# A fused attention and FFN kernel with a written issue order: every engine's order rewritten, and one wait named in the last pair's results

## The chip, the cores and the metric

The kernel runs on one core of one Trainium2 chip, as a single program. The metric is the device time of one execution in microseconds (us); the kernel before stands at the median of three runs. The core's engines are TensorE (PE; PEld is its weight load), ScalarE (ACT), VectorE (DVE), GpSimd (POOL) and SyncE (SP), whose queue issues nearly all of the DMAs. Each engine works through its own instruction stream in order, and an instruction that waits for a semaphore holds up everything behind it on that engine.

## The reference

```python
batch, n_heads, seq, head_dim = (8, 8, 576, 64)
n_pack = 32
...
    p_packed = sm_attn(p, k, v)
    out = sm_attn(q, p_packed, p_packed)
...
    x = np.ascontiguousarray(attn_out.transpose(0, 2, 1, 3)).reshape(B * S, H * D)
...
    h = x @ w_in
    g = 0.5 * h * (1.0 + erf(h * inv_sqrt2))
    return (g @ w_out).astype(np.float32)
```

All 576 keys and values of a head are first packed into 32 rows by a softmax attention with the 32 given queries p; then the 576 queries attend to these 32 rows (`sm_attn` is a scaled softmax attention). The result, 4608 tokens of 512, goes through w_in (512 x 2048), an exact gelu and w_out (2048 x 512).

## The kernel before, in words

**Units.** The eight batches are taken in four pairs, and the 2048 hidden columns in four quarters; a pair and a quarter make a unit, u = 0 to 15 (pair u // 4). For a unit the hidden products (`hidden_steps`, L1656, tiles h_n, eight to a unit, 12 matmuls of 128x288 each) fill a PSUM buffer of the ring `wide`, ACT takes the gelu out of it (L1681, in units of pair 0 L1688) and so frees the buffer, and the output products follow. Pair 0 uses plain output products (L1718 to L1720). Pairs 1 to 3 use a scheme with seven products instead of eight: the mixed operands a22, a11, s2, s3, s1, s4, a12, each multiplied in two halves of six matmuls of 128x512 (`mixed_steps`, L1907). Of the 576 rows of a batch 512 go that way; the other 64 are the edge (`edge_rows`, L1718 to L1720), one product with the weights k0 and k1, one with k2 and k3.

**Weights.** Each unit of pairs 1 to 3 loads eight weight tiles of 512 KB from DRAM (`load_one`, L1871): the plain k0 to k3 (names ws_... in DRAM) and the combined a22, s2, s3, s1 (names wx_...). They go through four buffers, in the order a22, k0, k1, s2, s3, s1, k2, k3; a load waits for the buffer that it takes. All of them are issued on SP's queue, between the loads of the next pair's attention: K and Q in four parts each (L860, tiles in_k and in_q), V (L918 and L926, a pair of DMAs), p (L936, two parts), and the w_in words (L1402). During pair 0 the weights are also decoded on ACT and DVE, from raw words that SP fetches (L1433, L1437; tiles wraws), cut into combined weights (fetched back at L1517) and stored (L1541, L1546).

**Attention of the next pair** runs between these products: scores (L973), transposes of the exponentials (e1Tm, L1077; they take a buffer of `wide` too), transposes of p (pTm, L943), packed rows (pp, L1164), and the pair's w_in product (wps, L1567).

**The last pair's results.** In unit 15 DVE adds or subtracts each PSUM half into four sums m4, c11, c12, c22 (`evict`, L1940); the product a22 goes into m4 with a subtraction. `results` then starts the task that transposes a sum back (DVE, L2079) and stores it (L2016); for c12 and c11 the transposes run on PE (L2025).

**What sets the order.** All of this is written as tasks that hand out operations (`Op`) for an engine and wait for events of others. A dry run numbers the operations. `TURNS` holds, for each of PE, ACT, DVE, POOL and DMA (the SP queue), a list of these numbers, 2431 in all, and the builder takes exactly the next number of each list:

```python
key = next(iter(ready), None) if self.dry else turns[engine][n] if n < len(turns[engine]) else None
if key in ready and self.issuable(ready[key][0]):
    op, go_on, begin = ready.pop(key)
...
else:
    if engine == PE and self.idle and self.idle():
```

The last line is `keep_warm` (L1625): where PE has nothing to issue during the first 150 us of the builder's clock, it puts in a fill matmul on a tile of zeros.

Of the kernel before, what the change touches and what calls it, by code (L numbers as in the profile page):

```python
# [132 lines left out]
        "56 57 62 64 63 53 83 61 82 80 81 114 120 101 68 119 100 96 95 97 94 135 86 93 72 146 71 73 123 121 169 "  # L133
        "129 132 131 136 115 151 152 209 164 165 144 184 225 143 200 116 142 249 153 333 203 348 444 217 226 "
        "449 451 363 454 371 455 464 466 470 564 471 566 473 474 475 572 487 492 498 501 579 573 580 588 595 "
        "322 600 603 604 606 323 607 610 612 614 452 615 622 625 629 585 633 643 654 644 665 634 646 658 657 "
        "671 669 681 685 693 537 538 708 680 722 684 731 514 738 740 692 744 749 704 751 755 650 651 757 759 "
        "763 766 417 418 769 772 773 777 779 781 783 784 785 788 792 795 720 797 802 803 807 818 798 805 810 "
        "813 823 831 687 837 838 849 688 694 855 695 846 861 718 868 876 879 884 854 886 889 860 689 892 728 "
        "895 696 898 899 900 901 641 642 902 903 690 904 905 697 906 907 742 760 743 908 909 866 910 912 914 "  # L140
        "916 767 918 924 927 938 925 919 926 933 934 941 942 949 950 957 956 963 969 962 975 981 982 983 968 "
        "984 986 821 820 988 991 811 812 994 997 998 999 1000 1001 1002 1003 1004 1005 1006 1007 974 1008 1010 "
        "1012 1015 1018 1033 1035 1038 1034 1037 1042 1047 1053 922 1057 1058 1068 923 1078 1093 1063 1066 1105 "
        "1071 1112 1082 1121 1102 1132 1109 1141 1115 1151 1080 1129 1161 1178 1163 1136 1193 1147 1203 1076 "
        "1075 1215 1238 1134 1244 1254 1176 1175 1267 1156 1144 1279 1169 1296 1185 1309 1206 1207 1322 1200 "
        "1335 1276 1350 1209 1359 1166 1235 1367 1249 1379 1260 1250 1388 1261 1242 1403 1277 1275 1405 1292 "
        "1248 1411 1329 1328 1251 1423 1262 1311 1426 1315 1252 1263 1269 1433 1317 1439 1326 1448 1319 1455 "
        "1282 1368 1369 1464 1331 1470 1341 1475 1355 1483 1489 1362 1496 1514 1428 1519 1372 1522 1449 1528 "
        "1434 1532 1460 1538 1466 1545 1472 1552 1542 1443 1477 1555 1486 1561 1572 1491 1576 1590 1511 1600 "
        "1622 1535 1630 1635 1553 1639 1543 1643 1558 1649 1567 1659 1574 1668 1583 1677 1596 1683 1690 1665 "  # L150
        "1664 1698 1709 1541 1722 1695 1614 1742 1627 1753 1672 1679 1765 1703 1702 1772 1687 1777 1692 1780 "
        "1656 1786 1705 1799 1747 1748 1820 1716 1828 1835 1670 1739 1850 1862 1794 1746 1873 1789 1801 1790 "
        "1802 1891 1795 1818 1899 1757 1912 1792 1826 1821 1922 1839 1840 1936 1830 1783 1946 1804 1842 1956 "
        "1854 1966 1791 1808 1803 1866 1972 1833 1927 1979 1988 1888 1994 1847 1895 1997 1901 1900 1999 1906 "
        "2014 1957 2019 1964 2026 1921 2032 1928 2038 1968 2047 1975 2060 1940 2065 2044 2071 2012 2081 2087 "
        "2016 2099 2107 2045 2021 2117 2136 2029 2145 2148 2064 2153 2067 2158 2077 2036 2163 2085 2167 2093 "
        "2172 2104 2178 2111 2187 2192 2043 2198 2203 2174 2175 2211 2229 2133 2236 2242 2185 2247 2170 2189 "
        "2251 2194 2262 2200 2270 2205 2277 2176 2284 2226 2291 2299 2260 2259 2305 2312 2231 2318 2331 2239 "
        "2334 2340 2274 2344 2249 2349 2279 2353 2283 2357 2288 2361 2293 2364 2302 2366 2368 2307 2370 2373 "
        "2263 2376 2378 2315 2380 2382 2384 2386 2351 2388 2390 2394 2399 2402 2355 2407 2410 2412 2415 2414 "  # L160
# [3 lines left out]
        "154 167 55 58 59 173 160 92 76 105 65 90 178 88 99 126 89 75 182 91 118 125 113 238 104 106 109 139 "  # L164
        "110 117 141 102 159 130 245 128 193 145 108 134 147 133 122 187 214 138 172 212 171 188 158 253 192 "
        "263 166 204 0 155 148 124 176 347 350 196 362 201 286 237 366 459 370 207 374 382 386 213 565 384 567 "
        "383 219 571 224 491 497 500 503 575 331 578 587 584 342 581 330 229 586 336 589 235 621 425 628 593 "
        "356 596 632 535 624 364 536 426 676 656 241 659 668 244 672 679 545 549 250 698 683 691 255 701 703 "
        "427 257 647 719 649 662 664 705 260 412 713 726 428 430 423 421 674 266 729 732 269 809 433 822 439 "
        "814 273 824 836 839 845 711 278 712 850 853 282 724 725 857 288 859 483 865 734 737 870 291 715 872 "  # L170
        "648 484 652 295 494 717 764 765 485 874 504 298 881 771 776 486 507 932 301 940 935 948 768 943 955 "
        "951 511 961 958 967 964 793 973 970 827 829 806 976 540 856 541 979 980 893 542 1036 1041 887 1043 "
        "1046 1048 543 1052 1055 1056 928 1060 1067 929 1062 1065 1079 1092 1077 1098 1084 1104 1090 1070 1111 "
        "1113 1069 1081 1085 1120 1101 1131 1095 1108 1133 1100 1110 1114 1074 1140 1128 1116 617 1150 1135 "
        "1130 1138 1146 1148 1152 618 1155 1157 1088 1160 1086 1167 1172 1189 1186 1165 1171 1168 1173 1184 619 "
        "1183 1204 1199 1205 1201 1230 1231 1188 1208 1210 1290 1240 1234 1236 1241 1256 1270 1271 1247 1258 "
        "1280 1293 620 1285 1286 1284 1303 1306 1259 1288 1272 1314 1316 1318 1300 1274 1440 1324 1325 1360 "
        "1336 1337 1305 1330 1332 1340 1345 1354 1357 1409 1361 1374 1435 1412 1371 1376 1408 1414 1419 1384 "
        "1459 1462 1442 1456 1465 1427 1471 1473 1457 1476 1547 1430 1485 1478 1487 1490 1493 1510 1520 1512 "
        "1516 1621 1539 1634 1636 1638 1524 1629 1557 1526 1559 1548 1642 1647 1533 1566 1658 1648 1662 1573 "  # L180
        "1575 1537 1582 1676 1667 1678 1595 1585 1597 1625 1613 1619 1673 1671 1682 1637 1641 1626 1628 1632 "
        "1700 1701 1686 1688 1712 1710 1646 1657 1691 1704 1706 1715 1743 1744 1661 1759 1760 1738 1769 1717 "
        "1740 1745 1807 1750 1756 1758 1811 1813 1810 1768 1775 1825 1824 1767 1832 1836 1829 1831 1788 1797 "
        "1841 1817 1892 1853 1806 1855 1865 1930 1887 1815 1889 1868 1935 1845 1846 1894 1903 1856 1859 1933 "
        "1905 1909 1924 1916 1958 1963 1932 1965 1967 1938 1939 1989 1952 1974 1976 1954 1981 1991 2053 1983 "
        "2015 2017 2020 2055 2023 2028 2039 2030 2042 2147 2151 2034 2135 2137 2066 2068 2157 2152 2160 2050 "
        "2076 2084 2086 2162 2040 2166 2169 2054 2171 2092 2058 2177 2103 2105 2110 2186 2132 2094 2144 2179 "
        "2134 2114 2180 2181 2146 2150 2156 2141 2188 2190 2161 2193 2199 2201 2204 2225 2165 2206 2230 2227 "
        "2233 2265 2264 2248 2238 2240 2253 2255 2244 2278 2280 2267 2282 2272 2287 2289 2292 2294 2301 2303 "
        "2306 2314 2316 2309 2332 2336 2328 2338 2345 2348 2420 2426"  # L190
    ),
    DVE: (
        "156 175 161 60 183 77 74 69 54 181 195 98 103 170 111 179 66 70 78 189 210 194 79 23 107 67 112 216 85 "
        "84 87 162 137 127 177 140 186 24 206 149 150 231 163 174 197 233 223 198 232 236 275 218 281 252 185 "
        "302 373 208 355 234 211 221 215 242 248 310 369 460 400 531 496 559 380 222 395 259 230 267 388 390 "
        "240 280 243 569 33 34 289 465 577 335 583 247 294 594 339 458 251 591 300 432 592 479 602 258 663 308 "
        "262 43 313 435 677 611 558 268 707 318 515 276 710 639 327 436 748 279 750 754 756 44 328 557 716 283 "
        "721 337 667 666 670 730 429 438 678 441 290 344 794 787 736 791 293 832 686 796 349 819 296 828 359 "
        "299 372 709 844 852 304 381 888 891 309 489 389 635 739 894 897 636 864 314 875 741 653 399 655 319 "
        "490 746 747 878 404 778 911 493 913 325 885 409 915 752 946 499 753 917 762 789 329 761 804 939 416 "  # L200
# [2010 lines left out]
```

## Time and profile before

| | |
|---|---|
| median of 3 runs | 700.88 us (699.51 to 701.84) |
| the profiled execution | 700.08 us, its span 698.2 us, granted TensorE clock 0.998 |
| PE busy | 684.7 us, 98% of the span |
| DVE, ACT, POOL busy | 519.2, 382.8, 318.1 us |
| DMA | 148.72 MB in 191326 packets, 146720 of them under 512 B |

The span runs from the first instruction to the last. Three views carry the reading. The chain of waits follows the work that ended last back to the start, and gives shares by engine and line. The waits of PE list for which line of which other engine or DMA it stood still, in total, how often and the longest. The timeline gives runs of like instructions with the start and, in brackets, the idle time ahead of one and what ended it; a DMA row on SPq is the issue alone, not the transfer.

### The profile page before, as it was taken

What the parts mean: (1) busy time and instruction counts of PE and PEld (TensorE: products, weight loads), DVE (VectorE), ACT (ScalarE), POOL (GpSimd) and SP (SyncE); (2) the same over time, 40 slices, a digit from 0 to 9 for tenths busy, and PEclk for the clock granted to TensorE, in tenths of its full rate; (3) what the DMA queues carried; (4) which work ended last, traced back from release to release, by engine and by line L of the source; (5) the groups of instructions that cost most, each with busy time, mean ns of one, the idle gap of its engine ahead of it and who ended that gap; (6) DMA issues with size and microseconds to landing.
All of it is one profiled execution on the core that took longest, in us unless ns stands there. A gap on an engine that the chain in (4) does not pass through costs nothing.

```text
span 698.2 us, 13293 instructions
## 1 busy us (share of the span) xinstructions
PE 684.7 (98%) x5157; PEld 559.1 (80%) x5157; DVE 519.2 (74%) x720; ACT 382.8 (55%) x601; POOL 318.1 (46%) x298
## 2 busy tenths in 40 slices
PE   9999999999999999999999999999999999999996
PEld 7768787887878797778787887787878798878984
DVE  5789878887897627878897837677989844656684
ACT  5886776765654754564665364355545464433330
POOL 4558764574440775043055815215141935242461
PEclk9999999999999999999999999999999999999999
DMA  9979999999829999999534499999825556514355
GB/s 339 339 258 208 278 278 252 193 331 287 291 83 333 311 199 242 249 236 242 168 121 181 131 195 269 171 229 240 232 92 176 155 144 193 222 61 164 109 174 142
DMA packets 191326, 148.72 MB, mean 213 GB/s; under 512 B 146720, under 2 KB 160032, under 8 KB 191264
## 3 DMA queue, kind: packets, MB, share of 16 engines
q1 hardware_dynamic: 188608, 146.83, 75.8%
q10 hardware_dynamic: 2656, 1.05, 0.6%
q8 instruction: 41, 0.67, 0.4%
q14 instruction: 21, 0.17, 0.1%
HBM read 113.25 MB, written 34.60 MB: 212 GB/s over the span
## 4 chain that ended last, share of the span: by engine, by line
PE 78%; DMA 8%; SPq 4%; DVE 4%; ACT 3%; issue 1%; ACTq 1%; DVEq 0%
PE o L1907 27%; PE h L1656 23%; PE o L1718 4%; PE o L1720 4%; PE o L1719 4%; PE wps L1567 4%; SPq L860 3%; PE o L1625 2%; PE h L1647 2%; DMA wx_s<-memory 2%; DMA rounded<-ws 2%; PE s L973 1%; PE pp L1164 1%; DMA p<-in_p_dram 1%; DMA rounded<-wx_s 1%
## 5 line engine op out<-in xcount | busy, mean ns | idle before, releaser
L1907 PE MATMUL o<-rounded 128*128 128x512 f32 (+1 forms) x1014 | 255.3, 393 | 3.2 <-DMA rounded<-ws 1.8
L1907 PEld LDWEIGHTS o<-rounded 128*128 128x128 f32 x1014 | 182.2, 188 | 50.2 <-issue 6.6
L1656 PEld LDWEIGHTS h<-a2T,wp 128*128 128x128 f32 x1440 | 202.3, 188 | 11.8 <-ACT memory L1681 2.2
L1656 PE MATMUL h<-a2T,wp 128*128 128x288 f32 x1440 | 210.7, 296 | 0.3 <-ACT memory L1681 0.3
L1858 DVE TENSOR_TENSOR rounded<-memory,rounded 128x1024 fp32r<-128x1024 f32 x82 | 112.2, 1376 | 42.8 <-ACT rounded L1852 36.5
L1852 ACT CAST rounded<-memory 128x1024 fp32r<-128x1024 f32 x84 | 87.9, 1052 | 99.3 <-PE o L1907 73.0
L1768 POOL TENSOR_TENSOR memory<-memory 128x1024 f32<-128x1024 f32 x36 | 91.6, 2544 | 93.9 <-ACT memory L1681 75.4
L1952 DVE TENSOR_TENSOR memory<-o,memory 128x512 f32<-128x512 f32 x124 | 82.3, 682 | 42.9 <-PE o L1907 37.9
L1681 ACT ACTIVATE memory<-h 128x576 f32<-128x576 f32 x96 | 61.4, 652 | 61.9 <-PE h L1656 55.8
L1781 POOL TENSOR_TENSOR memory<-memory 128x1024 f32<-128x1024 f32 x12 | 30.7, 2556 | 117.1 <-ACT memory L1681 93.2
L1718 PE MATMUL o<-rounded 128*128 128x512 f32 x176 | 72.2, 410 | 0.0
L1720 PE MATMUL o<-rounded 128*128 128x512 f32 x176 | 69.0, 392 | 0.0
L1719 PE MATMUL o<-rounded 128*128 128x512 f32 x176 | 68.7, 390 | 0.0
L1583 DVE TENSOR_TENSOR wp<-wps,wp 128x1024 fp32r<-128x1024 f32 x30 | 36.5, 1216 | 14.7 <-ACT wp L1578 14.7
L1718 PEld LDWEIGHTS o<-rounded 128*128 128x128 f32 x176 | 33.1, 188 | 12.9 <-issue 4.3
L1578 ACT CAST wp<-wps 128x1024 fp32r<-128x1024 f32 x30 | 30.0, 1016 | 24.2 <-PE wps L1567 24.1
L1805 POOL CAST rounded<-memory 128x128 fp32r<-128x128 f32 x48 | 24.6, 514 | 38.6 <-ACT memory L1681 17.1
L882 DVE STREAM_TRANSPOSE memory<-memory 128x1152 f32<-128x1152 f32 x24 | 32.8, 1370 | 9.3 <-DMA memory<-in_k_dram 7.8
L1720 PEld LDWEIGHTS o<-rounded 128*128 128x128 f32 x176 | 33.0, 188 | 7.6 <-DVE rounded L1697 0.4
L1719 PEld LDWEIGHTS o<-rounded 128*128 128x128 f32 x176 | 33.1, 188 | 5.4
L1494 POOL TENSOR_TENSOR memory<-memory 128x512 int32<-128x512 int32 x16 | 21.6, 1353 | 28.9 <-DVE memory L1466 17.8
L1567 PE MATMUL wps<-memory,pp 64*32 64x512 f32 (+1 forms) x544 | 33.6, 573 | 0.3 <-ACT memory L1681 0.3
(156 smaller groups left out, 885.9 us busy)
## 6 DMA issues: line engine op xcount, KB each, us to landing
rounded<-ws SPq DMA_DIRECT2D x48, 512.0 KB, 4.6
rounded<-wx_s SPq DMA_DIRECT2D x36, 512.0 KB, 4.7
memory<-ws SPq DMA_DIRECT2D x24, 512.0 KB, 5.8
wraws<-in_moe_w_out_dram SPq DMA_DIRECT2D x16, 512.0 KB, 5.5
ws<-rounded SPq DMA_DIRECT2D x16, 512.0 KB, 5.4
memory<-in_v_dram SPq DMA_DIRECT2D x15, 512.0 KB, 6.2
memory<-in_k_dram SPq DMA_DIRECT2D x48, 144.0 KB, 5.9
memory<-in_q_dram SPq DMA_DIRECT2D x48, 144.0 KB, 6.7
```

Source lines behind the costliest of these rows:

```text
L1567: nc.tensor.matmul(t[r0:r0 + 32, hh, :m], lhsT=pp[b][rows, hh, r0:r0 + 32], rhs=wi[u, hh][rows, g, cols], start=True, stop=True)
L1583: yield Op(DVE, 1.22, step, lambda: nc.vector.tensor_tensor(lo, x, hi.bitcast(F32), ALU.subtract))
L1656: nc.tensor.matmul(t[:, half, :HALF], lhsT=w[:, wpart, ch, fc], rhs=a2T[b, ch][:, apart, half * HALF:(half + 1) * HALF], start=ch == 0 and ...
L1681: lambda: nc.scalar.activation(x[:, c % 2].rearrange("p (a n) -> p a n", a=2), t[:, :, :HALF], AF.Gelu), table="gelu")
L1718: nc.tensor.matmul(t, lhsT=g[0], rhs=w[:, 0], start=first, stop=False)
L1719: nc.tensor.matmul(t, lhsT=g[0], rhs=w[:, 1], start=False, stop=False)
L1720: nc.tensor.matmul(t, lhsT=g[1], rhs=w[:, 0], start=False, stop=last)
L1768: return Op(POOL, 2.4, 0, lambda: nc.gpsimd.tensor_tensor(of(x), of(y), of(z), op))
L1852: o = op[u, m] = yield Op(ACT, 1.04, 0, lambda o: nc.scalar.copy(o[:, 0], x), [(ops, f"op_{u}_{m}")])
L1858: engine, cost, 0, lambda: on(engine).tensor_tensor(o[:, 1], x, o[:, 0].bitcast(F32), ALU.subtract), port=True)
L1907: nc.tensor.matmul(t[:, cols], lhsT=x[:, wpart], rhs=o[:, part, q, cols], start=first and q == 0 and wpart == 0 and part == 0, stop=q == 1 ...
L1952: yield Op(DVE, 0.685, 0, lambda: nc.vector.tensor_tensor(to(), x, to(), ALU.add))
```

## The change

The change has two parts. In `results` of the last pair two waits are added: the tasks that transpose the sums start only after both subtractions of a22 have been handed out. And all five lists of `TURNS` are replaced by permutations of themselves; operations, their numbers and their code stay. The rows of the lists are left out here but for the first and last.

```diff
 TURNS = {
     PE: (
-        "56 57 62 64 63 53 83 61 82 80 81 114 120 101 68 119 100 96 95 97 94 135 86 93 72 146 71 73 123 121 169 "
-        "129 132 131 136 115 151 152 209 164 165 144 184 225 143 200 116 142 249 153 333 203 348 444 217 226 "
...
+        "1962 2006 2118 2143 2127 2119 2125 2120 2220 2121 2122 2123 2221 2124 2212 2213 2219 2214 2215 2216 "
+        "2217 2218 2319 2320 2326 2321 2322 2323 2324 2325 2403 2359 2408 2424 2423 2429 2430"
     ),
 }
...
                 macs.give(of("u3"))
                 yield combine("c12", "c12", "c22", ALU.add)
                 fire(merged["c12"])
+                for h in range(2):
+                    yield evicted[NU - 1, MIXED.index("a22"), h]
                 for x, j, v, name in (("s3", 0, 0, "m4"), ("s1", 0, 1, "c22"), ("s4", 1, 1, "c12"), ("a12", 1, 0, "c11")):
                     yield evicted[NU - 1, MIXED.index(x), 0]
                     start({"s4": first_turned, "a12": last_turned}.get(x, result)(pr, j, v, name, x))
```

One line is added to `TURNS` and three lines of code in all shift what follows: L1907 of the kernel before is L1908 of the changed one.

**SP's queue in unit 9.** wx_1_s2, wx_1_s3 and wx_1_s1 are that unit's combined weights, ws_1_2 to ws_1_4 its k0, k1 and k2; x4 is one load in four parts. Before:

```order
L1871 DMA rounded_86<-ws_1_2_1049 128x1024
L1871 DMA rounded_86<-ws_1_3_1089 128x1024
L936 DMA p_6_4569<-in_p_dram 128x2x64 x2
L860 DMA memory_83<-in_k_dram 32x36x32 x4
L1871 DMA rounded_86<-wx_1_s2_101 128x1024
L860 DMA memory_83<-in_k_dram 32x36x32 x4
L1871 DMA rounded_86<-wx_1_s3_102 128x1024
L860 DMA memory_83<-in_q_dram 32x36x32 x4
L1871 DMA rounded_86<-wx_1_s1_103 128x1024
L1871 DMA rounded_86<-ws_1_4_1212 128x1024
```

After:

```order
L1872 DMA rounded_86<-ws_1_3_1107 128x1024
L1872 DMA rounded_86<-wx_1_s2_101 128x1024
L861 DMA memory_83<-in_k_dram 32x36x32 x4
L1872 DMA rounded_86<-wx_1_s3_102 128x1024
L861 DMA memory_83<-in_k_dram 32x36x32 x4
L1403 DMA memory_83<-ws_3_0_1855 128x1024
L1403 DMA memory_83<-ws_3_1_1953 128x1024
L1872 DMA rounded_86<-wx_1_s1_103 128x1024
L861 DMA memory_83<-in_q_dram 32x36x32 x4
L1872 DMA rounded_86<-ws_1_4_1228 128x1024
```

Each of the three combined weights now stands ahead of the four-part load that it stood behind; the load of p_6 stands earlier than the rows shown.

**SP's queue in units 5 and 6.** The names are those of the weights in DRAM: wx_1_s1, ws_1_4 and ws_1_5 are s1, k2 and k3 of unit 5, wx_2_a22 to wx_2_s3 and ws_2_2, ws_2_3 belong to unit 6. Before:

```order
L1871 DMA rounded_86<-wx_1_s1_103 128x1024
L1402 DMA memory_83<-ws_3_1_1946 128x1024
L860 DMA memory_83<-in_q_dram 32x36x32 x4
L1871 DMA rounded_86<-ws_1_4_1212 128x1024
L1871 DMA rounded_86<-ws_1_5_1240 128x1024
L1871 DMA rounded_86<-wx_2_a22_104 128x1024
L860 DMA memory_83<-in_q_dram 32x36x32 x8
L918 DMA memory_83<-in_v_dram 128x4x256
L926 DMA memory_83<-in_v_dram 64x4x64
L1871 DMA rounded_86<-ws_2_2_1566 128x1024
L1871 DMA rounded_86<-ws_2_3_1590 128x1024
L1541 DMA wx_3_s3_110<-memory_83 128x1024
```

There the next row is wx_2_s2, then wx_2_s3. After, from k0 of unit 6 on:

```order
L1872 DMA rounded_86<-ws_2_2_1576 128x1024
L861 DMA memory_83<-in_q_dram 32x36x32 x4
L1872 DMA rounded_86<-ws_2_3_1615 128x1024
L861 DMA memory_83<-in_q_dram 32x36x32 x4
L1872 DMA rounded_86<-wx_2_s2_105 128x1024
L1403 DMA memory_83<-ws_0_0_338 128x1024
L919 DMA memory_83<-in_v_dram 128x4x256
L927 DMA memory_83<-in_v_dram 64x4x64
L1403 DMA memory_83<-ws_0_1_291 128x1024
L919 DMA memory_83<-in_v_dram 128x4x256
L927 DMA memory_83<-in_v_dram 64x4x64
L1872 DMA rounded_86<-wx_2_s3_106 128x1024
```

Of the four Q loads of this pair three stood ahead of wx_2_s2 before, and all four do after; ahead of ws_1_4 stood one before, and two after. wx_2_s3 has moved behind two V loads.

**PE in unit 5.** The last row of each piece is the first half of product s4, the first use of k2 and k3; h_51 to h_53 are hidden products of unit 6, wps_7_0 belongs to unit 7. Before:

```order
L1907 MATMUL o_2_89<-rounded_86 128x512 x6
L1656 MATMUL h_51_3280<-a2T_2_0_2368,wp_6_0_2960 128x288 x6
L1656 MATMUL h_51_3280<-a2T_2_1_2460,wp_6_0_2960 128x288 x6
L1907 MATMUL o_1_88<-rounded_86 128x512 x6
L1567 MATMUL wps_7_0_0_3304<-memory_83,pp_2_1918 32x512 x8
L1907 MATMUL o_0_87<-rounded_86 128x512 x6
```

After:

```order
L1657 MATMUL h_51_3281<-a2T_2_0_2341,wp_6_0_2850 128x288 x6
L1657 MATMUL h_51_3281<-a2T_2_1_2441,wp_6_0_2850 128x288 x6
L1657 MATMUL h_52_3302<-a2T_3_0_2587,wp_6_1_2905 128x288 x6
L1657 MATMUL h_52_3302<-a2T_3_1_2561,wp_6_1_2905 128x288 x6
L1908 MATMUL o_2_89<-rounded_86 128x512 x6
L1657 MATMUL h_53_3335<-a2T_3_0_2587,wp_6_1_2905 128x288 x6
L1657 MATMUL h_53_3335<-a2T_3_1_2561,wp_6_1_2905 128x288 x6
L1908 MATMUL o_0_87<-rounded_86 128x512 x6
L1908 MATMUL o_1_88<-rounded_86 128x512 x6
```

h_52 and h_53 stood behind that product and stand ahead of it now; wps_7_0 stays ahead, further up.

Three more places, told without rows. In pair 0 the transposes e1Tm_2_0 stood on PE behind the hidden product h_20 and two output products more, and now stand one output product ahead of it; in ACT's list the copy of e1Tm_2_0 stands ahead of the gelu of h_20 (behind it before), and the decode of the first w_in word of quarter 3 stands ahead of the gelu of h_19 as before. In SP's queue a V load has moved from ahead of that word's fetch to behind it, and in unit 5 the p load of batch 4 (p_4) stands ahead of a four-part K load that was ahead of it. In unit 15 the first edge product stands two products earlier on PE, the second one. The changed program has 168 fill matmuls at L1625, the one before 163.

## Rows read from the trace of the kernel before

**Rows 1.** The page, part 1: busy time by engine, share of the span, instructions.

```profile
PE 684.7 (98%) x5157; PEld 559.1 (80%) x5157; DVE 519.2 (74%) x720; ACT 382.8 (55%) x601; POOL 318.1 (46%) x298
```

**Rows 2.** The page, part 4: the chain that ended last, shares by engine.

```profile
PE 78%; DMA 8%; SPq 4%; DVE 4%; ACT 3%; issue 1%; ACTq 1%; DVEq 0%
```

**Rows 3.** Waits of PE: line, what it waited for: us in total, times, longest.

```profile
PE o L1907 <- DMA rounded<-ws: 1.8, 2, 1.6
PE o L1907 <- DMA rounded<-wx_s: 1.3, 2, 1.0
...
PE e1Tm L1077 <- ACT memory L1688: 0.9, 1, 0.9
PE pTm L943 <- DMA p<-in_p_dram: 0.6, 1, 0.6
...
PE wps L1567 <- ACT memory L1681: 0.3, 1, 0.3
PE h L1656 <- ACT memory L1681: 0.3, 1, 0.3
PE s L973 <- ACT memory L1681: 0.2, 1, 0.2
```

**Rows 4.** Stretches of 50 us: busy us by engine, PE clock, DMA share, GB/s.

```profile
250.00:300.00 50.00, 49.10 (x349) 38.21 (x347) 35.26 (x40) 24.22 (x38) 20.98 (x18) 1.00 1.09 238
...
400.00:450.00 50.00, 49.56 (x333) 40.19 (x331) 30.89 (x33) 26.25 (x39) 19.04 (x17) 1.00 1.05 220
```

**Rows 5.** Timeline of SP's queue in unit 9: start us, us, issue.

```profile
439.23 0.64 SPq L1871 DMA_DIRECT2D rounded<-wx_s  x1
439.96 4.21 SPq L860 DMA_DIRECT2D memory<-in_k_dram  x4
444.22 1.05 SPq L1871 DMA_DIRECT2D rounded<-wx_s  x1
```

**Rows 6.** Timeline of PE in unit 9, first half of product s3.

```profile
450.83 1.63 PE L1907 MATMUL o<-rounded 128*128 128x512 f32 x6 [1.02 <-DMA rounded<-wx_s]
```

**Rows 7.** Timeline of PE in unit 5, k3's part of product s4, then h_52.

```profile
301.53 0.97 PE L1907 MATMUL o<-rounded 128*128 128x512 f32 x3 [1.63 <-DMA rounded<-ws]
302.34 1.75 PE L1656 MATMUL h<-a2T,wp 128*128 128x288 f32 x12
```

**Rows 8.** Timeline of SP's queue in unit 5, ahead of and at k2 and k3.

```profile
285.53 8.36 SPq L860 DMA_DIRECT2D memory<-in_q_dram  x4
293.99 1.44 SPq L1871 DMA_DIRECT2D rounded<-ws  x2
```

**Rows 9.** Timelines of PE and ACT in pair 0 around h_20 and e1Tm_2_0.

```profile
139.98 1.75 PE L1656 MATMUL h<-a2T,wp 128*128 128x288 f32 x12
...
141.51 0.66 ACT L1445 ACTIVATE memory<-wraws 128x512 f32<-128x512 f32 x1 [2.62 <-DMA wraws<-in_moe_w_in_dram]
...
143.97 0.75 PE L1077 MATMUL e1Tm<-ident,memory 128*128 128x128 f32 x4 [0.88 <-ACT memory L1688]
```

**Rows 10.** Timeline from the start: 16 fill matmuls in a row.

```profile
15.58 1.91 PE L1625 MATMUL o<-still 128*128 128x256 bf16 x16
```

**Rows 11.** Timeline of SP's queue, units 5 and 6: Q loads and wx_2_s2.

```profile
296.00 10.61 SPq L860 DMA_DIRECT2D memory<-in_q_dram  x8
...
311.38 0.38 SPq L1871 DMA_DIRECT2D rounded<-wx_s  x1
...
321.32 6.92 SPq L860 DMA_DIRECT2D memory<-in_q_dram  x4
```

**Rows 12.** Tile wx_s from 309 to 337 us: DMA issue to landing.

```profile
DMA to landing us min/median/max: 5.0/5.9/7.1
```

**Rows 13.** Timeline of PE in unit 6: first half of product s2.

```profile
324.77 1.67 PE L1907 MATMUL o<-rounded 128*128 128x512 f32 x6
```

**Rows 14.** The page, part 6: DMA issues, KB each, median us to landing.

```profile
rounded<-ws SPq DMA_DIRECT2D x48, 512.0 KB, 4.6
...
memory<-in_k_dram SPq DMA_DIRECT2D x48, 144.0 KB, 5.9
memory<-in_q_dram SPq DMA_DIRECT2D x48, 144.0 KB, 6.7
```

219 rows, old and new, of the table TURNS are left out of this document.

## The prediction

> **What bounds the kernel now.** The page's first part comes first: PE is busy for 684.7 of 698.2 us [rows 1], so the other engines can be slow without cost as long as PE is fed. The chain that ended last agrees: 78% of it is PE's own work, 8% DMA and 4% SP's queue [rows 2]. No operation is added or taken away except five fill matmuls, so PE's work stays, and only its waits can change. The list of PE's waits is therefore the second view [rows 3]: weights from DRAM 1.8 and 1.3 us, transposes e1Tm behind ACT 0.9, p 0.6, and three short waits for the gelu, 0.3 + 0.3 + 0.2. Together that is 5.4 us, and no reordering can give back more, start and tail aside (neither has a row here that the change clearly shortens). The third view places the waits. The two stretches of 50 us in which PE is starved of weights show a DMA share of 1.09 and 1.05 [rows 4], that is, DMA engines with nothing to spare; the timelines there show which loads stood ahead on SP's queue.
>
> The profiled execution took 700.08 us, its span 698.2. The sum below is made against it and then put on the median of the runs, 700.88, which is 0.8 higher. A measurement of this kernel can tell about 0.3% from no change, 2.1 us: under 698.8 is faster, over 703.0 slower.
>
> **The change, part by part.**
>
> *The added waits: 0.* On DVE, which runs in order, both subtractions of a22 into m4 already stood ahead of the transposes of m4, so the wait names an order that was there. Behind it are queued only the starts of four tasks whose first operations need later products. It can't gain; it could cost only if the subtractions came late, and DVE has them from the first product of unit 15.
>
> *Unit 9: -1.3.* The first half of s3 stood still for 1.02 us [rows 6]. Its load was issued at 444.22, right after a four-part K load that held SP's queue from 439.96 for 4.21 us [rows 5]. Now s2, s3 and s1 each stand ahead of the load that they stood behind, so s3 can be issued some 4.2 us sooner, four times what it lacked. The K loads pay: each comes later by a weight's issue, 0.64 or 1.05 us [rows 5]. Their cover is that their scores stand behind product s3 and half of s1 in both orders; without it PE would wait the same microsecond there. Bounds: -1.3 (both waits) and 0 (engines full, landing unchanged). I take -1.3, as 4.2 is far from 1.0.
>
> *Unit 5: -1.6.* k3 was 1.63 us late [rows 7], because k2 and k3 were issued at 293.99, when a four-part Q load of 8.36 us had left the queue [rows 8]. PE now does h_52 and h_53 ahead of that product, at most 1.75 us each [rows 7], some 3.4 us together. Against that, two Q loads instead of one stand ahead of k2, while a K load and a V load have moved elsewhere. Bounds: -1.6 and 0; I take -1.6, since the PE side alone is twice the wait. In unit 15 the rest of the wait for ws, 1.8 - 1.6 = 0.2, goes because the edge products free their buffers sooner: -0.2, or 0.
>
> *p: -0.6.* Its load now stands ahead of a four-part K load, which is worth more than 4 us by the row of its like [rows 5]. Bounds -0.6 and 0.
>
> *Gelu waits: -0.4.* ACT's list is permuted too; of 0.8 us [rows 3] I count half. Bounds -0.8 and 0.
>
> *Pair 0, e1Tm and h_20: +0.5.* Here a wait changes hands. ACT stood 2.62 us for a raw weight word until 141.51, the gelu behind it freed the buffer late, and e1Tm_2_0 waited until 143.97 [rows 9]. In the new order e1Tm_2_0 goes ahead of h_20 and takes the buffer of an earlier gelu, so its 0.9 us go. But h_20, which started at 139.98 unhindered, then needs the buffer that e1Tm needed. It is reached at about 139.98 + 0.75 = 140.7, and if ACT is no faster it waits up to 143.97 - 140.7 = 3.3. Net, between -0.9 and 3.3 - 0.9 = +2.4; the middle is +0.75, and I take +0.5, because a V load no longer stands ahead of the word's fetch.
>
> *Start: +0.6.* Five fill matmuls more, 1.91/16 = 0.12 each [rows 10], mean PE waits 0.6 longer for its first inputs. Bounds 0 (they fill a gap that was already there) and +0.6.
>
> *Unit 6: +0.8.* This is what is late next. wx_2_s2 was issued at 311.38, and PE used it at 324.77 [rows 11, 13]. Now a fourth Q load stands ahead of it, which took 6.92 us when it came later [rows 11]: issue at about 318.3, landing 5.0 to 7.1 later [rows 12], 323.3 to 325.4, that is -1.5 to +0.6 against the use. One of the Q loads ahead may take 8.36 as in unit 5 [rows 8], which adds 1.4 to 2.0; a V load behind it delays s3 besides. Bounds 0 and 0.6 + 2.0 + about 0.4 = 3.0; I take +0.8, nearer the lower end: with the median landing of 5.9 it is in time.
>
> Sum: -1.3 - 1.6 - 0.2 - 0.6 - 0.4 + 0.5 + 0.6 + 0.8 = -2.2. The profiled execution would take 697.9 us, the median 698.7.
>
> **The rivals.**
>
> *Nothing new waits.* h_20 finds its buffer free (-0.9 instead of +0.5) and unit 6 is in time (0 instead of +0.8): -2.2 - 1.4 - 0.8 = -4.4, 696.5 us. For it: one order can be late where the other was early, and most of the loads moved in unit 6 still land by its use. Against: both places are thin by the rows above.
>
> *The waits for weights stay.* The engines, not the queue, may set the landings: with a share of 1.09 and 1.05 [rows 4] a load issued 4 us earlier just queues among more packets. A K or Q part of 144 KB took 5.9 or 6.7 us to land, a weight of 512 KB 4.6 [rows 14]; the small parts load the engines out of proportion, and both orders have all 96 of them. Then 1.3 + 1.6 + 0.2 = 3.1 come back and unit 6 is as it was, without its 0.8: -2.2 + 3.1 - 0.8 = +0.1, 701.0 us. Against it: the s3 of unit 9 follows a single K load, and PE restarts 6.6 us after s3's issue, so position in the queue did count there.
>
> The Trainium skill has the rule behind this rival, in "DMA: Bandwidth & Descriptors", section Specifications: a transfer needs pieces of at least 512 B for line rate. By that rule the engines' time is fixed by the pieces, whatever the order, and the sum would be this rival's 701.0; by the rows of the queue it is 698.7. The trace agrees with the rule as far as the 144 KB parts land later than the 512 KB weights; that order cannot help, no row shows.
>
> *Slower: the Q loads are slow in a row.* If each of the four-part Q loads holds the queue for 8.4 us as the one at 285.53 did, and not 10.61/2 = 5.3 as the pair at 296.00 [rows 8, 11], then s2 of unit 6 is issued 8.4 for the fourth load and 3.1 for a slower third one later, at 322.9. It lands at 330.0 with the longest landing of rows 12, 5.2 us after its use instead of 0.8: +4.4. And k3 of unit 5, now behind two of them, keeps its 1.6 us: -2.2 + 4.4 + 1.6 = +3.8, 704.7 us. It decides from where the two together exceed 2.2 + 2.1 = 4.3 us. For it: the stretch with share 1.09 lies just ahead, and the change puts more of these parts ahead of weights there. Against it: two Q loads in a row took 5.3 each.
>
> *The change doesn't do what it says.* Of the first part this holds, by the order: a wait that was there already. It is in the sum at 0, and the time is decided by the lists alone.
>
> **How the numbers follow.** The forecast, waits of units 5 and 9 and of p gone with a small price, has a chance of 0.50 and a range of its own from 697.4 to 700.0; three fifths of it lie below 698.8. Nothing new waits: 0.19. The waits stay: 0.18, within 0.3%. Slow Q loads: 0.13, nearly all of it slower. So faster 0.50 x 0.6 + 0.19 = 0.49, same 0.20 + 0.18 + 0.01 = 0.39, slower 0.12. The predicted time is the likeliest case's, 698.7. The range goes from 695.9, just under the second case, to 702.0, above the third; it leaves out the slow case and the outer ends of the bounds, under 2 in 10. The bounds all at one end would give 695.5 and 706.9.
>
> **What would show it.** In the profile after, the waits of PE should list no L1908 waiting for wx_s in unit 9 and none for ws in unit 5 over 0.3 us, and no pTm waiting for p. h_20 (L1657, near 141 us) should wait 0.5 to 2 us for ACT, and the first half of s2 in unit 6 up to 1 us. The first hidden product should start about 0.6 us later. The forecast is wrong if the waits for weights still come to 3 us in units 5 and 9, if one wait of over 3 us stands in unit 6, or if PE's list of waits is as long as before at other places.

## The result and the profile after

The changed kernel takes **693.27 us** (median of 4 runs, 692.73 to 694.01) against 700.19 of the kernel before on the same chip (698.12 to 701.84, 4 runs): a ratio of 0.9903, interval 0.9874 to 0.9933. It is faster by 6.9 us, three times the 2.2 that were forecast and below the range's lower end of 695.9. The sign was right, the size was not. A second set of 7 runs gave 693.59, ratio 0.9909 [0.9878, 0.9941].

The page of the changed kernel, parts 1, 3, 4 and 6 (its profiled execution took 694.01 us):

```profile
span 692.2 us, 13291 instructions
...
PE 682.7 (99%) x5162; PEld 561.3 (81%) x5162; DVE 521.0 (75%) x720; ACT 383.9 (55%) x601; POOL 321.7 (46%) x298
...
DMA packets 191326, 148.72 MB, mean 215 GB/s; under 512 B 146720, under 2 KB 160032, under 8 KB 191264
...
PE 93%; DMA 3%; SPq 1%; ACT 1%; DVE 1%; issue 0%; ACTq 0%
...
rounded<-ws SPq DMA_DIRECT2D x48, 512.0 KB, 4.5
...
memory<-in_k_dram SPq DMA_DIRECT2D x48, 144.0 KB, 5.2
memory<-in_q_dram SPq DMA_DIRECT2D x48, 144.0 KB, 6.4
```

Two things are to be read here beside [rows 1, 2]. The span is 6.0 us shorter, and PE's busy time fell too, from 684.7 to 682.7, with five matmuls more. So of the 6.0 some 2.0 is busy time and 4.0 is idle time (698.2 - 684.7 = 13.5 before, 692.2 - 682.7 = 9.5 after). And the chain that ended last is now 93% PE, where DMA and SP's queue held 12% of it.

PE's waits in the changed kernel: line, what it waited for, us in total, times, longest. They answer to [rows 3].

```profile
PE o L1626 <- DVE still L648: 1.0, 1, 1.0
PE o L1908 <- DMA rounded<-wx_s: 1.0, 1, 1.0
PE h L1657 <- ACT memory L1682: 0.7, 1, 0.7
PE o L894 <- DMA memory<-in_k_dram: 0.2, 1, 0.2
PE o L1908 <- DMA rounded<-ws: 0.2, 1, 0.2
```

The first row is the program's start, and the kernel before has it as well. Without it 2.1 us are left, where the list before held 5.8: the 5.4 of the prediction, and 0.4 at a second wait for p that stood among the left-out rows. The two stretches that were starved of weights, with the columns of [rows 4]:

```profile
250.00:300.00 50.00, 49.96 (x358) 39.96 (x357) 35.83 (x44) 27.01 (x43) 18.78 (x16) 1.00 1.01 223
400.00:450.00 50.00, 50.00 (x322) 42.09 (x322) 30.71 (x35) 23.73 (x36) 16.27 (x15) 1.00 1.06 229
```

PE is now busy for all of them, though the DMA share is still above 1 (1.09 and 1.05 before).

SP's queue and PE in unit 9, which answer to [rows 5, 6]:

```profile
429.00 0.38 SPq L1872 DMA_DIRECT2D rounded<-wx_s  x1
429.48 6.33 SPq L861 DMA_DIRECT2D memory<-in_k_dram  x4
435.99 0.86 SPq L1872 DMA_DIRECT2D rounded<-wx_s  x1
```

```profile
439.76 1.65 PE L1908 MATMUL o<-rounded 128*128 128x512 f32 x6
...
445.56 1.52 PE L1908 MATMUL o<-rounded 128*128 128x512 f32 x6
```

The load of s3 is issued at 435.99, 9.6 us ahead of its product at 445.56. Before, it was issued at 444.22 for a product at 450.83 that had waited. No product of unit 9 waits now.

Unit 6, SP's queue and then PE, beside [rows 11, 13]:

```profile
302.89 7.37 SPq L861 DMA_DIRECT2D memory<-in_q_dram  x4
...
311.08 4.67 SPq L861 DMA_DIRECT2D memory<-in_q_dram  x4
315.85 1.78 SPq L1872 DMA_DIRECT2D rounded<-wx_s  x1
```

```profile
304.04 1.84 PE L1657 MATMUL h<-a2T,wp 128*128 128x288 f32 x12 [0.67 <-ACT memory L1682]
...
321.66 1.63 PE L1908 MATMUL o<-rounded 128*128 128x512 f32 x6 [0.97 <-DMA rounded<-wx_s]
```

s2 is issued behind the fourth Q load, as forecast, and is 0.97 late.

Pair 0, PE and then ACT, beside [rows 9]:

```profile
139.18 0.64 PE L1078 MATMUL e1Tm<-ident,memory 128*128 128x128 f32 x4
...
140.46 1.75 PE L1657 MATMUL h<-a2T,wp 128*128 128x288 f32 x12
```

```profile
137.42 0.68 ACT L1446 ACTIVATE memory<-wraws 128x512 f32<-128x512 f32 x1
```

The word was there when ACT came to it, at 137.42 instead of 141.51 after a wait of 2.62. So neither e1Tm nor h_20 waits.

### The profile page after: what moved, and what is told of

The parts are those of the page before. It is cut to its first block, busy times and chain, and to the rows that moved or that the text cites. A ratio compares the mean times of both kernels' runs of the same rounds, so it can differ in the third digit from the quotient of the medians.

```text
span 692.2 us, 13291 instructions
## 1 busy us (share of the span) xinstructions
PE 682.7 (99%) x5162; PEld 561.3 (81%) x5162; DVE 521.0 (75%) x720; ACT 383.9 (55%) x601; POOL 321.7 (46%) x298
## 3 DMA queue, kind: packets, MB, share of 16 engines
q10 hardware_dynamic: 2656, 1.05, 0.6%
## 4 chain that ended last, share of the span: by engine, by line
PE 93%; DMA 3%; SPq 1%; ACT 1%; DVE 1%; issue 0%; ACTq 0%
PE o L1908 32%; PE h L1657 26%; PE o L1719 6%; PE o L1721 6%; PE o L1720 6%; PE wps L1568 4%; PE o L1626 2%; PE h L1648 2%; PE s L974 2%; DMA memory<-in_k_dram 1%; PE pp L1165 1%; DMA rounded<-ws 1%; PE e1Tm L1078 1%; DMA rounded<-wx_s 1%; SPq L2019 1%; PE o_edge L1721 1%
## 5 line engine op out<-in xcount | busy, mean ns | idle before, releaser
L1908 PE MATMUL o<-rounded 128*128 128x512 f32 (+1 forms) x1014 | 250.3, 392 | 1.2 <-DMA rounded<-wx_s 1.0
L1908 PEld LDWEIGHTS o<-rounded 128*128 128x128 f32 x1014 | 183.7, 188 | 47.6 <-issue 5.0
L1657 PEld LDWEIGHTS h<-a2T,wp 128*128 128x128 f32 x1440 | 199.7, 188 | 9.2 <-ACT memory L1682 1.9
L1657 PE MATMUL h<-a2T,wp 128*128 128x288 f32 x1440 | 204.8, 295 | 0.7 <-ACT memory L1682 0.7
L1859 DVE TENSOR_TENSOR rounded<-memory,rounded 128x1024 fp32r<-128x1024 f32 x82 | 107.6, 1320 | 35.9 <-ACT rounded L1853 35.7
L1806 POOL CAST rounded<-memory 128x128 fp32r<-128x128 f32 x48 | 25.2, 526 | 43.8 <-PE o L1720 30.2
```

Of the source, the lines that this page charges most:

```text
L1657: nc.tensor.matmul(t[:, half, :HALF], lhsT=w[:, wpart, ch, fc], rhs=a2T[b, ch][:, apart, half * HALF:(half + 1) * HALF], start=ch == 0 and ...
L1859: engine, cost, 0, lambda: on(engine).tensor_tensor(o[:, 1], x, o[:, 0].bitcast(F32), ALU.subtract), port=True)
L1908: nc.tensor.matmul(t[:, cols], lhsT=x[:, wpart], rhs=o[:, part, q, cols], start=first and q == 0 and wpart == 0 and part == 0, stop=q == 1 ...
```

## The experiments

All medians are in us; each ratio is to the kernel before in runs of the same chip. What an edit of the lists says is in the numbers of `TURNS`. All kernels below but order_only have the added wait.

**The added wait, and the lists without it.**

```diff
 # wait_only: the lists of before, and
+                for h in range(2):
+                    yield evicted[NU - 1, MIXED.index("a22"), h]
 # order_only: the lists of the change, without these lines
```

> The kernel before with the two named waits and its own lists. The instructions of every engine are those of before, so: no difference, 0.997 to 1.003 of before. If the named wait does something that the instructions don't show: up to 0.990.

> The changed lists without the two named waits: the instructions of every engine are then those of the changed kernel, so this is also a second measurement of it on this chip. If the lists bring all of the gain: 0.990 of before as the changed kernel, with PE waits of some 2 us after the start. If the named wait has a share: slower than the changed kernel by that share, over 2 us to be seen.

The wait alone: 700.25, ratio 0.9983 [0.9955, 1.0011]. The lists alone: 692.90, ratio 0.9892 [0.9860, 0.9925]. In both the instructions of every engine come in the same order as in the kernel that they were made from. The change is its lists, and the wait names an order that was there. wait_only therefore also shows what a second execution of before's order looks like. Its waits of PE:

```profile
PE o L1907 <- DMA rounded<-ws: 2.6, 3, 1.5
PE o L1907 <- DMA rounded<-wx_s: 1.3, 2, 1.1
...
PE h L1656 <- ACT memory L1681: 0.9, 1, 0.9
PE o L943 <- DMA p<-in_p_dram: 0.8, 1, 0.8
PE h L1656 <- ACT memory L1688: 0.5, 1, 0.5
```

With four more of 0.2 to 0.4 the list comes to 7.2 us, start aside, where the same order showed 5.8 [rows 3]: weights and gelus are waited for longer, e1Tm's 0.9 has shrunk to 0.2. How much PE waits, and for what, differs from execution to execution of one order.

**One stretch of the lists at a time.** Four kernels take the order of the change in one stretch and that of before elsewhere: up to 220 us, 220 to 370, 370 to 520, and the rest (by the times for which the operations were planned).

```diff
 # h1_pair0: PE's places 1 to 255, ACT's to 223, DVE's to 246, POOL's and DMA's to 122 and 123
-        "56 57 62 64 63 53 83 61 82 80 81 114 120 101 68 119 100 96 95 97 94 135 86 93 72 146 71 73 123 121 169 "
+        "62 63 64 57 53 56 83 80 81 82 61 114 119 120 101 68 100 96 97 95 94 135 86 93 72 146 123 169 129 121 "
...
 # h2_mid: PE's places 266 to 379; h3_late: 382 to 498; h4_tail: 501 to 610; the other lists alike
```

> The changed order on all five engines for the operations of the first 220 us (pair 0), the order before after that. Theory (the gain is the sum of PE waits that lie in each stretch, of weight-product blocks joined on PE, and of the start): -1.6 us of waits around 95, 143 and 162 us, -0.35 for one pair of w_in products put side by side, +0.6 for the later start: about -1.3 against before. Rival (the gain comes as a whole, because the DMA engines are full and a load sent earlier only helps if all of them are): 0, or +0.6.

> The changed order for the operations from 220 to 370 us (units 4 to 6 and part of 7), the order before elsewhere. Theory of the sum by stretches: waits of 3.9 us go (224, 275, 292, 299.5 us among them), 2.1 come (303 and 320 us), one pair of w_in products joined: about -2.0. Rival (only the whole order helps): within 0.5 of before.

> The changed order for the operations from 370 to 520 us (units 8 to 10 and parts beside them), the order before elsewhere. Theory of the sum by stretches: the waits at 438, 443, 449.5 and 471 us, 2.1 in all, go and none comes: about -2.1. Rival (only the whole order helps, since the DMA share is 1.05 there): within 0.5 of before.

> The changed order for the operations from 520 us to the end, with the wait that the change names. Theory of the sum by stretches: -0.1 of waits, -0.35 for one pair of w_in products joined, -0.3 in the tail: about -0.7. Rival (the wait named in the last pair's results is what brings the gain): -5 or more here, and nothing in the other three.

Against 701.52 (34 runs) they gave 698.53 (0.9960 [0.9934, 0.9987]), 705.64 (1.0047 [1.0019, 1.0076]), 702.04 (0.9997 [0.9961, 1.0033]) and 706.41 (1.0066 [1.0037, 1.0095]). The sum of the four differences is -3.0 + 4.1 + 0.5 + 4.9 = +6.5, where the whole change is -6.9. None of the three later stretches is shown to be faster (-2.0, -2.1 and -0.7 were expected), and two are slower. Their traces have waits that neither whole order shows; these are the likely reason that the four do not add up to the change. Timelines of PE, of h2_mid behind its first cut and at its second, and of h4_tail behind its cut:

```profile
227.10 6.64 PE L1657 MATMUL h<-a2T,wp 128*128 128x288 f32 x48 [0.94 <-ACT memory L1682]
...
234.72 1.83 PE L1657 MATMUL h<-a2T,wp 128*128 128x288 f32 x12 [0.99 <-ACT memory L1682]
...
366.24 1.66 PE L1908 MATMUL o<-rounded 128*128 128x512 f32 x6 [1.38 <-DVE memory L1953]
```

```profile
549.53 0.53 PE L1719 MATMUL o<-rounded 128*128 128x512 f32 x1 [3.81 <-DVE memory L1953]
```

h3_late has four waits for weights inside its own stretch, from 444.81 to 486.67, of 2.3 us together. Only the first stretch reads cleanly. In the trace of h1_pair0 PE has no wait over 0.2 us up to 270 us, start aside, and k2 and k3 of unit 5 still wait, 1.30 and 2.10: the order there is worth some 3 us (by the interval 0.9 to 4.6), more than the 1.3 expected. How the rest divides over the later stretches stays open.

**Unit 9, undone in the change and done alone.**

```diff
 # u9_undo, DMA: s2, s3 and s1 (1603 to 1605) again behind the four-part loads
-        "... 1684 1608 1603 1654 1604 1669 1731 1732 1605 1735 "
+        "... 1684 1608 1654 1603 1669 1604 1731 1732 1735 1605 "
 # before_u9, DMA of before: the reverse
-        "... 1608 1650 1654 1603 1669 1604 1735 1605 1606 1731 "
+        "... 1608 1650 1603 1654 1604 1669 1605 1735 1606 1731 "
```

> The changed kernel with one thing undone on SP's queue: in unit 9 s2, s3 and s1 each stand behind the four-part load again that they stood behind before. Theory (place in the queue decides, and each load of four parts holds it for 4 to 6 us): the waits for wx_s in unit 9 come back, 1.0 to 1.6 us against the order-only kernel. Rival (the DMA engines set the landing): no wait there, within 0.5 of it.

> The kernel before with one part of the change alone: in unit 9 s2, s3 and s1 each go ahead of the four-part load that stood ahead of them. Theory: the waits of 438 to 450 us go, 1.6 us by the trace of before; and where a run of before has a longer wait there, followed by PE at half its clock as in the kernel with unit 9 undone (2.8 us of wait, then 5 us at 0.50), more: 1 to 3 us faster than before. Rival (only the whole order helps): within 0.7 of before.

u9_undo gave 696.46, ratio 0.9946 [0.9922, 0.9971]: 3.6 more than order_only in the same set, where 1.0 to 1.6 were expected. Its timeline of PE and its stretches of 5 us (columns as in [rows 4]):

```profile
439.93 1.63 PE L1908 MATMUL o<-rounded 128*128 128x512 f32 x6 [1.75 <-DMA rounded<-wx_s]
...
454.57 2.90 PE L1908 MATMUL o<-rounded 128*128 128x512 f32 x6 [2.83 <-DMA rounded<-wx_s]
```

```profile
450.00:455.00 5.00, 2.17 (x14) 1.96 (x13) 1.29 (x2) 2.23 (x3) 0.00 (x0) 0.86 1.06 304
455.00:460.00 5.00, 5.00 (x39) 2.53 (x39) 0.00 (x0) 1.02 (x4) 0.00 (x0) 0.50 0.97 164
460.00:465.00 5.00, 5.00 (x32) 4.61 (x32) 3.48 (x6) 2.16 (x5) 0.00 (x0) 0.95 0.84 273
```

s2 and s1 wait again, 1.75 and 2.83 us, each behind a four-part load; and behind the second wait the granted clock is 0.50, the 1.2 GHz level, for 5 us: the six matmuls behind it take 2.90 us where six took 1.63 behind the first wait. So the wait is paid for twice. The profiled run is one of the longest of the 12 (699.59, granted clock 0.994); the others have 0.995 to 0.999, so the 3.6 of the median need not have such a stretch in it. before_u9, the same exchanges in the old lists, gave 700.75, ratio 0.9993 [0.9966, 1.0019]. Unit 9 has no wait in its trace either, but others stand in the list of PE:

```profile
PE o L1719 <- DMA rounded<-ws: 2.1, 1, 2.1
PE wps L1568 <- ACT e1T L1096: 1.5, 1, 1.5
PE s L974 <- ACT memory L1689: 1.2, 1, 1.2
```

The exchange does locally what the prediction said. Alone it brings nothing that can be measured.

**Unit 5: h_52 ahead of k3's part.**

```diff
 # b_h52, PE of before
-        "1335 1276 1350 1209 1359 1166 "
+        "1335 1276 1209 1350 1359 1166 "
```

> The kernel before with another part alone: on PE the hidden product h_52 goes ahead of the first half of product s4 in unit 5, which waited 1.63 us for k3. Theory (the wait is covered by 1.6 us of work that was to be done anyway): the wait at 300 us goes, 1.5 us faster than before. Rival (it is put off): PE waits about as long at 320 us, for the softmax of batch 4, whose steps hang on the same loads: within 0.7 of before.

698.78, ratio 0.9969 [0.9943, 0.9995]: 2.2 us by the ratio, 0.4 to 4.0 by its interval. In its trace the wait of 1.63 [rows 7] is down to 0.16, at the same place. One exchange of two neighbours on PE carries that term.

**Unit 6: s2 ahead of the last Q load.**

```diff
 # u6_s2, DMA of the change
-        "... 1298 1223 1313 1218 1397 "
+        "... 1298 1223 1218 1313 1397 "
 # u6_both: that, and on ACT a cast of unit 6 behind two gelus
-        "... 1234 1210 1241 1236 1256 "
+        "... 1234 1241 1236 1210 1256 "
```

> The changed kernel with its two remaining PE waits attacked: on SP's queue s2 of unit 6 goes ahead of the last Q load (it lacked 0.97 us at 321.66), and on ACT the cast for product a22 of unit 6 goes behind the two gelus that follow it (PE stood 0.67 us for them at 304.04). If these waits lie on the path that sets the end: 1.6 to 1.9 us faster than the order-only kernel, near 691.5 on a scale where the changed one has 693.3. Rival (the time is given back a little later, at k1 or s3 of unit 6 or at the scores of the Q load that is put back): within 0.7 of the order-only kernel.

> The changed kernel with one exchange on SP's queue: s2 of unit 6 ahead of the last Q load of its pair; ACT's list as in the changed kernel. In the run with both edits the wait for s2 was gone, and the cast moved on ACT had cost more than the gelus gained. If the s2 wait (0.97 and 1.4 us in two traces) lies on the path: about 1 us faster than the order-only kernel, 0.988 of before. Rival (the Q load put back is then late, or s3 behind it): no faster, within 0.7 of it.

> The exchange at s2 of unit 6 again, beside the changed kernel on the same chip: 0.7 to 1.5 us faster than it if the wait for s2, 1.0 and 1.4 us in two traces of the changed kernel, lies on the path; the rival is a difference of under 0.5.

u6_both was a miss: 695.07, ratio 0.9936 [0.9915, 0.9957], slower than order_only by 2.2 instead of faster. Its DVE and PE show a new wait:

```profile
303.41 2.58 DVE L1859 TENSOR_TENSOR rounded<-memory,rounded 128x1024 fp32r<-128x1024 f32 x1 [1.70 <-ACT rounded L1853]
305.91 0.68 DVE L1834 TENSOR_TENSOR memory<-o,memory 128x512 f32<-128x512 f32 x1
```

```profile
306.64 4.38 PE L1908 MATMUL o<-rounded 128*128 128x512 f32 x18 [2.45 <-DVE memory L1834]
```

The 0.67 that the gelu's hidden product waits was taken away, but DVE now stands still for 1.70 until the cast that moved for it is done, and its instruction then takes 2.58, where it takes 1.18 in the changed kernel (at 302.79); why it takes longer is open. The subtraction queued behind it frees an accumulator, so PE waits 2.45. The 12 runs have a granted clock of 0.993 to 0.997, those of order_only 0.998 to 0.999; in a run of 695 us each 0.001 is 0.7 us (an estimate from these numbers), so a part of the 2.2 is probably clock. Without the cast's move, u6_s2 gave 692.29, ratio 0.9874 [0.9838, 0.9911], and then 692.78, 0.9899 [0.9870, 0.9928]. Its s2 does not wait. In the second set it is 0.8 below after_again; in the first no kernel with the change's lists ran beside it (its ratio there is 0.9874, that of order_only in another set 0.9892). The intervals overlap, so it is the fastest version seen, but not one shown to be faster. In the profile of the second set s1 of unit 9 waited 1.03 in its stead (at 450.58).

**The blocks of wps.** These are matmuls with 64 rows and tiles of 32 columns, while those around them use the whole array. Timelines of PE at the blocks of unit 1, before (the second block stands at 78.77) and changed:

```profile
74.47 0.39 PE L1720 MATMUL o<-rounded 128*128 128x512 f32 x1
74.79 1.09 PE L1567 MATMUL wps<-memory,pp 64*32 64x512 f32 x16
75.81 0.50 PE L1718 MATMUL o<-rounded 128*128 128x512 f32 x1
76.15 0.39 PE L1719 MATMUL o<-rounded 128*128 128x512 f32 x1
```

```profile
74.28 0.40 PE L1721 MATMUL o<-rounded 128*128 128x512 f32 x1
74.60 1.95 PE L1568 MATMUL wps<-memory,pp 64*32 64x512 f32 x32
76.48 0.50 PE L1719 MATMUL o<-rounded 128*128 128x512 f32 x1
76.82 0.39 PE L1720 MATMUL o<-rounded 128*128 128x512 f32 x1
```

From its start to the next start a block of 16 takes 1.02 us, and 32 in a row take 1.88. The products on either side are slower too: 0.32 and 0.34 from start to start, where one among its like takes 0.23. With what they lose a block of 16 costs 1.22 and 32 in a row 2.09 (by unrounded times), so a join saves 2 x 1.22 - 2.09 = 0.35. The change joins three pairs that stood apart (units 1, 5 and 13). It also parts a pair of blocks half as wide (64x256): before, they took 1.02 together (at 48.60), after, 0.57 and 0.59 (at 46.37 and 49.08), 0.14 more. split3 parts the three again, split_wps all ten joined pairs of the changed kernel, each by one other operation.

```diff
 # split3, PE of the change (split_wps: these and seven pairs more)
-        "... 322 323 595 ... 923 922 1068 ... 2045 2044 2099 "
+        "... 322 595 323 ... 923 1068 922 ... 2045 2099 2044 "
```

> The changed kernel with its ten adjacent pairs of w_in products (wps, 32 matmuls in a row) split again: the operation that follows a pair on PE goes between its two halves; the other lists stay. Nothing else moves. In the traces a block of 16 costs PE 1.22 us and one of 32 costs 2.09, so if that is a cost of entering and leaving a block, ten splits cost 10 x 0.35 = 3.5 us against the order-only kernel. Rival (the price of a block is only the pitch of its matmuls, and the joined pairs gained nothing): within 0.7 of the order-only kernel.

> The changed kernel with only the three pairs of w_in products split that the change had joined (units 1, 5 and 13). If joining pays 0.35 us each: 1.05 us slower than the changed kernel, and the rest of the gain, some 5 to 6 us, is waits. Rival (the ten splits cost more than their blocks because they moved the waits too, and three cost nothing): within 0.5 of it.

> The changed kernel once more, as the mark for the two others on this chip: 0.988 to 0.992 of before, with waits of PE of 2 to 4 us after the start, at other places than in its first two traces or of other sizes.

split_wps: 697.53, ratio 0.9960 [0.9939, 0.9982], 4.6 above order_only in the same set. split3: 694.55, ratio 0.9927 [0.9901, 0.9954], 0.96 above after_again in the same set; the size is the expected one, but the intervals overlap. after_again itself lists 1.4 us of waits, start aside, under the 2 to 4 expected. What separates these kernels is part 1 of the page, of order_only, split3, split_wps and wait_only in turn:

```profile
PE 682.0 (98%) x5162; PEld 560.6 (81%) x5162; DVE 520.5 (75%) x720; ACT 384.2 (55%) x601; POOL 321.8 (46%) x298
```

```profile
PE 684.0 (99%) x5162; PEld 561.0 (81%) x5162; DVE 520.8 (75%) x720; ACT 384.5 (56%) x601; POOL 323.3 (47%) x298
```

```profile
PE 685.7 (99%) x5162; PEld 559.2 (80%) x5162; DVE 520.7 (75%) x720; ACT 384.2 (55%) x601; POOL 321.5 (46%) x298
```

```profile
PE 684.3 (98%) x5157; PEld 559.2 (80%) x5157; DVE 517.7 (74%) x720; ACT 382.4 (55%) x601; POOL 317.2 (45%) x298
```

PE is busy for 682.0 to 682.7 us in the five profiles that have the joins and nothing else undone (the change twice, order_only, u6_s2 twice), for 684.0 without the three, for 685.7 without the ten, and for 684.0 to 684.7 in the four with the lists of before or one exchange in them. (u9_undo, with all the joins, has 685.2: matmuls at half the clock are busy for longer.) So PE's busy time depends on the order, by 1.3 to 2.0 us for these three joins; 3 x 0.35 = 1.05 of it is what the starts explain. A second part is the ends of waits. A 128x512 product is listed as busy for 0.39 us, though the next one can start after 0.23, so where PE waits behind it, some 0.16 of the wait is listed as busy time; split3 lists four waits, after_again two.

## Why the prediction was right and wrong

**The added waits, 0: right.** wait_only and order_only settle it, and with it the part of the rival that the change doesn't do what it says.

**Units 9 and 5, p: right by place.** All these waits are gone from the places that the prediction named (in one of the five profiles of such lists, the second of u6_s2, s1 of unit 9 waits 1.03). For unit 5 b_h52 shows the mechanism alone, at 2.2 where -1.6 was taken. For unit 9 u9_undo shows it in the new order, at 3.6 where -1.3 was taken; before_u9 shows that in the old order it is worth nothing measurable. p was not tried by itself.

**Unit 6, +0.8: the right size, in part by luck.** s2 is 0.97 late, 1.41 in order_only, and not at all in after_again. The prediction had the load issued at about 318.3 for a use at 324.77. It was issued at 315.85, and PE came to it at 321.66 - 0.97 = 320.69, 4.1 us sooner than before, with the same matmuls ahead of it but for the five fills: what is saved further up brings the use forward, and the sum of terms left that out. The two errors cancelled for the most part.

**Gelu, -0.4: too much.** The three waits are gone from their places, but one of 0.7 stands at 304.04: net -0.1.

**Pair 0, +0.5: wrong.** It came to -0.9. Its condition "if ACT is no faster" failed: ACT could decode the word 4.09 us earlier, as its fetch was issued at 132.32 instead of 135.22, and h_20 found its buffer free. Whether the V load that now stands behind the fetch did this wasn't tried.

**Start, +0.6: not borne out.** The first hidden product starts at 43.8 in the profile after against 43.1, but at 43.3, 43.3, 43.6 and 42.6 in four more with 168 fill matmuls, and at 43.0 in wait_only. That is mostly variation.

**The step that failed** is the ceiling: "PE's work stays, and only its waits can change", with "5.4 us, and no reordering can give back more". Both halves fell. PE's busy time shrank by 2.0, and two things that the prediction put at nothing are in it. Neighbouring blocks of wps cost less than separate ones; the order of PE had three new neighbours, and I priced the same operations at the same time: 3 x 0.35 less 0.14 is 0.9. And a list of waits leaves out some 0.16 us of each wait (k3's 1.63 is 1.80 when the usual distance from start to start is taken off the one seen): with ten waits listed before and four after, start aside, that is an estimated 1.0. Five more fill matmuls, 0.6 by the prediction's price, go the other way, so some 0.7 of the 2.0 is not explained. Nor was 5.4 all that was listed: it was the list of one execution, with a second wait for p of 0.4 left out, which is gone too; the same order waited 7.2 in wait_only.

For the profiled pair the sum closes. The start's 0.6 has to come out of the forecast -2.2, as PE's busy time has the fill matmuls in it: -2.8. Less 1.4 in pair 0, less 2.0 of busy time, less 0.4 at p, plus 0.3 at the gelus, 0.2 in unit 6 and 0.4 for two short new waits (k and a weight) is -5.7, and the tail behind PE's last matmul is 0.3 shorter: -6.0, as measured. The step from there to the medians' -6.9 is the spread of single executions: 690.9 to 695.4 in 17 of the changed lists, and the profiled one, at 694.01, was the slowest of its four.

**The rivals.** "Nothing new waits" (696.5) was half right, in pair 0, and came nearest. "The waits for weights stay" (701.0) is refuted. The DMA share of those stretches is 1.01 and 1.06, the packets are the same to the last one, and PE doesn't wait there. In unit 9 the place in SP's queue decided (u9_undo), in unit 5 the order of PE is enough (b_h52). The rule of the Trainium skill that stood beside it ("DMA: Bandwidth & Descriptors", section Specifications: pieces of at least 512 B for line rate) agrees with the 144 KB loads that still land after 5.2 and 6.4 us, where a 512 KB weight took 4.5; it did not set the time. "Slow Q loads" (704.7) did not come: the two in front of s2 held the queue for 7.37 and 4.67 us, and k3 of unit 5 was in time.

What stays open: how the 6.9 divides over the stretches behind 220 us, since the cuts make waits of their own; some 0.7 us of PE's busy time; and whether u6_s2 is faster at all.

## What to carry to other kernels

An engine that is busy for 98% can still lose work by a mere reordering: look for neighbours of the same small shape that the new order joins or parts, and price a block with what the matmuls on either side of it lose. A list of waits from one execution is one draw; before it serves as a ceiling, take a second profile of the same order, and add what the modelled end of the matmul ahead hides of each wait. And before a wait is taken away by moving an instruction, look at what is queued behind it on its own engine: in u6_both 0.67 us were saved on PE and 2.45 lost.

## What was not expected of the hardware

- **One wait can be paid for twice.** In u9_undo PE stood still for 2.83 us, with a granted clock of 1.00 in the 10 us up to 450; from 450 to 455, the wait in it, the clock was 0.86 on the mean; the 5 us behind that were granted 0.50, that is 1.2 GHz, and 32 score matmuls took 2.17 us there (at 457.40), where they took 1.20 at 436.97. Behind the 2.10 us of h1_pair0 the stretch from 301 to 306 had 0.66. It is not the length of the wait alone: behind the 2.45 us of u6_both and the 2.15 of before_u9 (at 264.02) the clock stayed at 1.00.
- **A block of 64-row matmuls costs something at its ends.** With what the products beside it lose, 16 of them cost 1.22 us and 32 in a row 2.09. The transposes e1Tm show nothing like it, with 0.60 for one and 1.20 for two, counted the same way.
- **Executions of one order differ, and not by as much in every order.** The lists of before gave 696.5 to 703.9 in 12 runs of wait_only, those of the change 690.9 to 695.4 in 17: the changed order is not only faster but less spread. That loads which come just in time make the spread is likely, and not shown.
